# Six even weight places between two attention layers, gelu as one ScalarE instruction, and a norm moved into the stage of w4

## The chip, the core and the metric

The kernel runs on one core of a Trainium2 chip. The core has TensorE (PE: matrix products; its weight loads are shown as PEld), VectorE (DVE), ScalarE (ACT), GpSimd (POOL) and SyncE (SP), and 16 DMA engines that bring data from HBM. All transfers of this kernel are issued on SP's queue, in the order in which the program planned them. The metric is device time in microseconds (us); less is better. The time of a kernel is the median of several runs, and beside it there is one execution that the hardware profiler recorded.

## The reference

A decode step for two sequences (B = 2, one new token each, width D = 576) through two layers. Each layer is an attention over a cache of 16384 keys and values with 32 heads of 128, followed by a block with a small mixing part and an MLP. Both layers use the same weights and the same caches.

```python
def layernorm(x, eps=1e-5): return (x - mean(x)) / sqrt(var(x) + eps)

def A(x):                       # attention, 2 x 32 heads, 16384 keys, Dh = 128
    q = (x @ wq).reshape(B, 1, 32, 128)
    p = softmax(q . k_cache * 128 ** -0.5)
    return (p . v_cache) @ wo   # wq [576, 4096], wo [4096, 576]

def Bmix(x):
    h = gelu(layernorm(x) @ w1)         # w1, w2 [576, 576]
    hs = shifted(h) @ w2                # one token: every shift leaves zeros
    x1 = x + hs
    return x1 + gelu(layernorm(x1) @ w3) @ w4   # w3 [576, 4608], w4 [4608, 576]

x = x + A(layernorm(x));  x = x + Bmix(layernorm(x))    # layer 1
x = x + A(layernorm(x));  x = x + Bmix(layernorm(x))    # layer 2
```

With one token the four shifted groups are all padding, so hs is a product of zeros with w2. The kernel computes it that way, once, and computes h of both layers at the end.

## The kernel before, in words

**Sizes.** There are 64 heads (2 sequences x 32), numbered 0 to 63. The keys of one head are a tile of 4 MB: 128 partitions, in each 128 blocks of 128 bf16 (32 KB). Its values are another such tile. Two layers read 1.09 GB in all. On-chip memory `mem` has six slots of one tile each, numbered 0 to 5.

**One head.** Of its 128 key blocks, half are transposed by TensorE in chunks of 8 blocks (`transposes`, L1225) into one of four PSUM banks `tps`, copied by ScalarE into one of three buffers `kt` (`evacuate`, L1237), and multiplied with q (`scores`, L1251). The other half is multiplied by VectorE with the broadcast q and summed (`dots`, L1271 and L1275). A maximum over partitions follows on GpSimd (L1291), the exponentials on ScalarE (`softmax_exp`, L1300 to L1306), and the products with the values on TensorE (`pv`, L1345). The work of head s is interleaved with the softmax and the value products of head s - 1. Most heads run in a loop.

**Carried heads.** Layer 2 begins with heads 62, 63 and 61. The keys and values of 62 and 63 stay in memory from layer 1 to layer 2, and so does part of head 61. For that the halves of K of heads 62 and 63 that VectorE used are transposed too, sixteen chunks that are written back in place: these are "turned" chunks (`turn`, with TensorE's transposes and, in `settle`, ScalarE's copies). Four of them are turned when head 63 begins, two after the products with w3, and ten behind the chunks named in the table `TURNS`. `park` transposes the first chunks of head 61's keys into the `kt` buffers (`PARKED` = 3), which frees the memory where they lay.

**The stage between the layers.** When attention of layer 1 is done, the products with wo, w3, w4 and (for layer 2) wq follow, each of about 5 MB of weights. Memory is nearly full of carried tiles, so the weights pass through *places*: four of 576 KB in slot 4 (`A[0]` to `A[3]`, where 72 value blocks of head 61 lay) and one, `B`, in slot 1 (where head 61's parked key chunks lay). The planner `Store` keeps transfers in a fixed order; a transfer is issued as soon as its place is free, and none overtakes another. A place is free when TensorE has used the piece in it. wo comes in 8 pieces, w3 in 7 (two of them 1152 KB), w4 in 10, wq in 8 (one of 1024 KB). `rows_projection` (L872) computes the products with wo and w4, `cols_chunk` (L751) and `cols_tail` (L768) those with w3 and wq.

**The dependences.** `layernorm` (L688 to L715) forms sums on VectorE, adds them over partitions with a product with ones (L695), takes a square root on ScalarE (L707) and scales. The first chunks of w3 and wq are multiplied with the raw x, so that they need not wait for the norm, and corrected later (`scaled`). In `z_projection` the norm for w1 (`layernorm("xb", ...)`) stands between the last whole chunks of w3 and its tail. Then z is summed (L906), and `gelu` takes three VectorE operations (L910, L911, L913), a sigmoid on ScalarE (L914) and one more on VectorE (L915). w4 needs its result. After wq, q is written at L814.

**Behind the stage.** `carried` scores heads 62, 63 and 61 from what lies in memory. The 72 value blocks of head 61 are fetched again in four pieces into slot 4, then the keys of head 0 in four quarters into slot 3 (where head 62's keys lay), then tiles of heads 1 and on as slots 5, 0, 2, 1 come free. SP's issues are all at L101.

Of the kernel before, what the change touches and what calls it, by code (L numbers as in the profile page):

```python
# [328 lines left out]
class KB:  # L329
# [42 lines left out]
    def _alloc(self):  # L372
# [23 lines left out]
        self.g_a = self.prod[:, 0:2 * MT * B].bitcast(FP32)  # L396
        self.g_b = self.prod[:, 2 * MT * B:4 * MT * B].bitcast(FP32)
# [14 lines left out]
        w = KT * NL * B  # L412
        hg = self.kt[0][:, :, :].rearrange("p j n -> p (j n)")
        self.hg = [hg[:, 2 * w * i:2 * w * (i + 1)].bitcast(FP32) for i in range(2)]
# [16 lines left out]
    def plan_tile(self, t, u, slot, cuts=()):  # L431

        b, hh = u % self.B, u // self.B
        src = (self.K if t == "k" else self.V)[b, hh].rearrange("(p j) d -> p (j d)", p=128)
        cuts = [0, *cuts, self.NB]
        for a, z in zip(cuts[:-1], cuts[1:]):
            self.plan_piece(t, u, slot, src, a, z - a)

    def plan_piece(self, t, u, slot, src, a, n):
        sem = f"tile{slot}" if n == self.NB else f"piece{slot}_{a}_{n}"  # L440
        self.store.plan((t, u, a, n), sem, slot * self.TILE + 256 * a, 256 * n,
                        [(lambda m: m, src[:, a * 128:(a + n) * 128])])
# [60 lines left out]
    def plan_all(self):  # L503
# [12 lines left out]
        for (t, u), slot in zip(tiles, place):  # L516
# [12 lines left out]
        self.cuts["w4", 0] = [(h + a, h + b, at) for h in (0, MT // 2)  # L529
                              for a, b, at in zip(g[:-1], g[1:], (A[2], A[3], B, A[0], A[1]))]  # L530
        self.plan_rows("wo", 0, self.wo, self.cuts["wo", 0])
        h = MT // 2
        self.plan_cols("w3", 0, self.w3, [(0, 0, h, A[3]), (0, h, MT, B), (1, 0, MT, A[0]), (2, 0, MT, A[2]),
                                          (3, 0, h, B), (3, h, MT, A[0]), (4, 0, MT, A[1])])
        self.plan_groups("w4", 0, self.w4, self.cuts["w4", 0])
        h = H // 2
        self.plan_cols("wq", 1, self.wq, [(0, 0, H, A[2]), (1, 0, h, B), (1, h, H, A[1]), (2, 0, h, A[0]),
                                          (2, h, H, A[2]), (3, 0, h, A[3]), (3, h, H, B), (4, 0, H, A[1])])

        b, hh = third % self.B, third // self.B  # L540
        for i in (0, 2, 3, 1):
            self.plan_piece("v", third, 4, self.V[b, hh].rearrange("(p j) d -> p (j d)", p=128), i * self.GONE // 4,
                            self.GONE // 4)
        tiles = self.tile_order(1)
        place = [(3, 4, 5, 0, 2, 1)[i % 6] for i in range(len(tiles))]
        for i, (t, u) in enumerate(tiles):
            if (t, u) != ("v", third):
                self.plan_tile(t, u, place[i], (quarter, half, half + quarter) if i == 0 else
                               (half,) if i == len(tiles) - 1 else ())
# [134 lines left out]
    def layernorm(self, sk, src, dst, dk, after=None):  # L684
# [9 lines left out]
        tot = self.mps[:, 0:2 * B]  # L694
        self.pe(lambda pe: pe.matmul(tot, lhsT=self.ones_f[:, :],  # L695
                                     rhs=self.stat[:, :, :].rearrange("p a b -> p (a b)"), start=True, stop=True),
                reads=["stat", "ones_f"], writes=["mps"])
        if after:
# [3 lines left out]
                reads=["mps"], writes=["mv"])  # L702
# [37 lines left out]
    def cols_chunk(self, w, l, k, out, pk, n, rhs, rk, cols, first, last=False):  # L740
# [15 lines left out]
        if l == (1 if w == "wq" else 0):  # L756
            self.turn(self.TURNS.get((w, k), 0))

# [35 lines left out]
    def q_projection(self, l):  # L794
# [7 lines left out]
                       after=lambda: self.cols_chunk("wq", l, 0, acc, [ak], n, self.raw[:, 0, 0:w], "raw", cols, True, True))  # L802
# [56 lines left out]
    def rows_projection(self, w, l, rhs, rk):  # L859
# [4 lines left out]
        for i, (a, b, _) in enumerate(cuts):  # L864
# [11 lines left out]
            self.store.release(nm)  # L876
            if l == 0:
                self.turn(self.TURNS.get((w, i), 0))

    def z_projection(self, l):  # L880
# [6 lines left out]
        chunk = lambda k: self.cols_chunk("w3", l, k, acc, [ak], MT, self.raw[:, k, :], "raw", cols, k == 0, k == R - 1)  # L887
# [16 lines left out]
        self.layernorm("xb", self.xb, self.xn2[:, l, :, :], "xn2")  # L904
# [4 lines left out]
    def gelu(self, src, sk, a, ak, b, bk, dst, dk):  # L909
        self.dv(lambda e: e.tensor_tensor(out=a, in0=src, in1=src, op=ALU.mult), reads=[sk], writes=[ak])  # L910
        self.dv(lambda e: e.tensor_scalar(out=a, in0=a, scalar1=GELU_C, scalar2=1.0, op0=ALU.mult, op1=ALU.add),  # L911
                reads=[ak], writes=[ak])
        self.dv(lambda e: e.tensor_tensor(out=b, in0=a, in1=src, op=ALU.mult), reads=[ak, sk], writes=[bk])  # L913
        self.act(lambda e: e.activation(out=a, in_=b, func=ACT.Sigmoid, scale=GELU_S), reads=[bk], writes=[ak])  # L914
        self.dv(lambda e: e.tensor_tensor(out=dst, in0=src, in1=a, op=ALU.mult), reads=[sk, ak], writes=[dk])  # L915

    def gelu_z(self):
        self.gelu(self.z, "prod", self.g_a, "prod", self.g_b, "prod", self.gT, "prod")
# [28 lines left out]
    def attention(self, l):  # L947
# [11 lines left out]
        for s in range(self.CARRY + 1 if l else 0, U):  # L959
# [7 lines left out]
            if still and s == U - 1:  # L967
                self.unturned = [(v, b) for v in o[U - self.CARRY:] for h in range(2)
                                 for b in range(h * self.BP + self.PB, (h + 1) * self.BP, self.CH)]
                self.unsettled = []  # L970
                self.turn(4)
            self.landed(l, "k", u, both=turning)
            after = self.early(l, s - 1)
            for c in range(2 * n):
# [24 lines left out]
                elif s >= 1:  # L999
# [28 lines left out]
        if leave < U:  # L1028
            self.park(o[leave - 1])
# [28 lines left out]
    def turn(self, n, settle=True):  # L1058

        for _ in range(n):  # L1060
            u, b = self.unturned.pop(0)
            self.transposes(0, u, b, 0, self.chunk)
# [10 lines left out]
    def park(self, u):  # L1073

        n = self.PARKED
        self.store.carve(("k", u, 0, self.NB), [self.CH * (i + 1) for i in range(n)] + [self.BP])
        for c in range(n):
            self.transposes(0, u, c * self.CH, c, self.chunk)
            self.store.release(("k", u, c * self.CH, self.CH))
            self.unsettled.append((self.chunk, (None, self.kt[c][:, :, :].rearrange("p j n -> p (j n)"), [("kt", c)])))  # L1080
            self.chunk += 1

    def carried(self, o):
# [13 lines left out]
        def fresh(c):  # L1097
            self.transposes(1, o[2], c * self.CH, c, self.chunk)
            self.evacuate(c, self.chunk, (None, self.kt[c % self.NKT][:, :, :].rearrange("p j n -> p (j n)"),
                                          [("kt", c % self.NKT)]))  # L1100
            self.chunk += 1
# [13 lines left out]
        still(1, 0, 6)  # L1115
        self.softmax_exp(1, 0, o[0])
        dots(1)
        third(3)
        fresh(5)
        still(1, 6, 11)  # L1120
        third(4)
        fresh(6)
        still(1, 11, N)
        self.softmax_max(1, 1, o[1])
# [316 lines left out]
```

## Time and profile before

| quantity | before |
|---|---|
| median of 3 runs | 2559.52 us (2559.41 to 2559.8) |
| the profiled execution: its time / its span | 2557.7 us / 2556.0 us |
| bytes read from HBM | 1092.37 MB, 427 GB/s over the span |
| VectorE / TensorE / ScalarE busy | 74% / 63% / 47% of the span |
| DMA, slices 20 and 21 of 40 (1214 to 1342 us) | 414 and 359 GB/s |

How to read it: the span is cut into 40 equal slices of 64 us; each digit is a busy share in tenths, and GB/s is what the DMA engines moved. A row of a stage gives its start and end, its length, then for each engine its busy time and instructions, TensorE's granted clock, the DMA share and GB/s. In the timeline a row is start, duration, engine, line, operation, out<-in, and in brackets the idle time before it and what ended it. In a view of waits a row is engine, what waited, who ended the wait, total us, times and the longest. The chain of waits is the work that ended last, followed back; its rows are start, duration, what.

### The profile page before, as it was taken

The numbers are of one execution on the slowest core, as the hardware profiler recorded it, in microseconds if no ns is written. First come the engines' busy times: TensorE is split into PE (matmuls) and PEld (weight loads), VectorE is DVE, ScalarE is ACT, GpSimd is POOL, SyncE is SP. The second block draws the span as 40 slices with busy tenths as digits, with TensorE's granted clock in tenths as the row PEclk, the third lists the DMA queues.
The fourth block names the chain that finished last, engine by engine and source line by source line (L and its number), as shares of the span: only waits on it lengthen the run. The fifth ranks groups of instructions, "written<-read, shape, count | busy, mean of one in ns | idle before, by whom it ended". The sixth has DMA issues, their size and how long they took to land.

```text
span 2556.0 us, 74895 instructions
## 1 busy us (share of the span) xinstructions
PE 1616.7 (63%) x34407; PEld 1582.5 (62%) x34407; DVE 1899.1 (74%) x2074; ACT 1200.7 (47%) x1808; POOL 52.5 (2%) x151
## 2 busy tenths in 40 slices
PE   4666666666666666665777666666666666666566
PEld 3666666656656666665667656666665666666566
DVE  5877777777777777777648777777777777777774
ACT  3544444544444454444435544454444445444442
POOL 0000000000000000000000000000000000000000
PEclk8555555555555555555655555555555555555655
DMA  9999999999999999999999999999999999999999
GB/s 410 430 430 433 431 431 432 432 431 431 432 431 432 431 432 433 431 432 432 414 359 427 433 431 431 433 431 432 432 430 434 430 432 433 431 431 432 431 433 388
DMA packets 46496, 1093.19 MB, mean 428 GB/s; under 512 B 5092, under 2 KB 6248, under 8 KB 11624
## 3 DMA queue, kind: packets, MB, share of 16 engines
q1 hardware_dynamic: 46440, 1092.40, 99.9%
q8 instruction: 41, 0.67, 0.1%
q14 instruction: 15, 0.12, 0.0%
HBM read 1092.37 MB, written 0.00 MB: 427 GB/s over the span
## 4 chain that ended last, share of the span: by engine, by line
DMA 66%; DVE 22%; PE 5%; issue 5%; SPq 1%; ACT 1%; DVEq 0%; POOLq 0%
DMA mem<-in_A_k_cache_dram 64%; DVE s_dve L1275 12%; DVE prod L1271 8%; PE tps L1225 2%; PE mps L1345 2%; DMA mem<-in_B_w_dram 2%; SPq L101 1%; PE sps L1251 1%; DMA mem<-in_A_wq_dram 1%; PE sps L1196 1%; ACT mem L1237 0%; DVE diag L1192 0%; DMA mem<-in_A_wo_dram 0%; DVE q_col L1189 0%; DVE l L1323 0%
## 5 line engine op out<-in xcount | busy, mean ns | idle before, releaser
L1237 ACT ACTIVATE kt<-tps 128x1024 bf16<-128x1024 bf16 x992 | 1003.0, 1023 | 878.4 <-PE tps L1225 862.0
L1275 DVE TENSOR_REDUCE s_dve<-prod 128x16 f32<-128x2048 bf16 x504 | 1152.1, 2286 | 17.3
L1225 PE MATMUL tps<-ident,mem 128*128 128x128 bf16 x8192 | 1000.2, 300 | 140.1 <-POOLq L202 134.8
L1271 DVE TENSOR_TENSOR prod<-mem,qb 128x2048 bf16<-128x2048 bf16 x504 | 616.7, 1224 | 533.1 <-POOLq L202 498.1
L1345 PE MATMUL mps<-p,mem 128*128 128x1 bf16 x16384 | 512.1, 165 | 549.6 <-POOLq L202 522.5
L1225 PEld LDWEIGHTS tps<-ident,mem 128*128 128x128 bf16 x8192 | 762.7, 136 | 149.8 <-POOLq L202 144.3
L1345 PEld LDWEIGHTS mps<-p,mem 128*128 128x128 bf16 x16384 | 488.2, 105 | 557.3 <-ACT p L1306 553.7
L1251 PEld LDWEIGHTS sps<-q_col,kt 128*128 128x128 bf16 x7936 | 399.6, 113 | 0.7 <-issue 0.5
L1251 PE MATMUL sps<-q_col,kt 128*128 128x1 bf16 x7936 | 387.8, 170 | 0.6 <-issue 0.4
L1196 PE MATMUL sps<-diag,ones_bf 128*128 128x128 bf16 x127 | 36.5, 288 | 194.1 <-DVE diag L1192 194.1
L1196 PEld LDWEIGHTS sps<-diag,ones_bf 128*128 128x128 bf16 x127 | 13.3, 105 | 204.3 <-DVE diag L1192 204.3
L1300 ACT ACTIVATE mx<-mx 128x1 f32<-128x1 f32 x128 | 26.1, 204 | 233.6 <-POOL mx L1291 233.6
L1199 ACT ACTIVATE qb<-sps 128x128 bf16<-128x128 f32 x127 | 35.2, 277 | 139.2 <-PE sps L1196 139.2
L1291 POOL PARTITION_ALL_REDUCE mx<-mx x128 | 50.1, 392 | 2450.7 <-DVE mx L1289 2321.5
L1237 ACT ACTIVATE mem<-tps 128x1024 bf16<-128x1024 bf16 x32 | 31.3, 1043 | 33.1 <-PE tps L1225 28.0
L1303 ACT ACTIVATE p<-s_dve,mx 128x64 bf16<-128x64 f32 x126 | 43.8, 348 | 4.1
L1306 ACT ACTIVATE p<-sps,mx 128x64 bf16<-128x64 f32 x128 | 37.7, 294 | 0.1
L1286 DVE TENSOR_REDUCE mx<-sps 128x1 f32<-128x64 f32 x128 | 27.6, 216 | 7.5 <-PE sps L1251 7.5
L872 PE MATMUL mps<-prod,mem 128*128 128x2 bf16 x680 | 22.1, 166 | 17.2 <-DMA mem<-in_B_w_dram 7.0
L872 PEld LDWEIGHTS mps<-prod,mem 128*128 128x128 bf16 x680 | 20.2, 104 | 19.5 <-DMA mem<-in_B_w_dram 7.8
L1192 DVE TENSOR_SCALAR diag<-ident,q_f 128x128 bf16<-128x128 bf16 x127 | 31.1, 245 | 0.0
L707 ACT ACTIVATE misc<-misc 128x2 f32<-128x2 f32 x8 | 2.4, 294 | 52.4 <-DVE misc L705 52.4
(122 smaller groups left out, 293.1 us busy)
## 6 DMA issues: line engine op xcount, KB each, us to landing
mem<-in_A_k_cache_dram SPq DMA_DIRECT2D x124, 4096.0 KB, 40.7
mem<-in_A_v_cache_dram SPq DMA_DIRECT2D x123, 4096.0 KB, 49.6
mem<-in_B_w_dram SPq DMA_DIRECT2D x9, 1152.0 KB, 33.4
mem<-in_B_w_dram SPq DMA_DIRECT2D x17, 576.0 KB, 7.3
mem<-in_A_v_cache_dram SPq DMA_DIRECT2D x3, 2048.0 KB, 40.4
mem<-in_A_wq_dram SPq DMA_DIRECT2D x5, 1024.0 KB, 7.0
mem<-in_A_wo_dram SPq DMA_DIRECT2D x8, 576.0 KB, 18.6
mem<-in_A_wq_dram SPq DMA_DIRECT2D x8, 512.0 KB, 6.9
```

The source lines that it names most:

```text
L872: ins = pe.matmul(self.mps[:, t * B:(t + 1) * B], lhsT=buf[:, o:o + 128], rhs=rhs(k), start=(k == 0 and t == 0), stop=(k == last), skip_gr ...
L1196: self.pe(lambda pe: pe.matmul(qps, lhsT=self.ones_bf[:, :], rhs=self.diag[:, :], start=True, stop=True, skip_group_check=True), reads=["o ...
L1199: self.act(lambda e: e.activation(out=self.qb[i][:, :], in_=qps, func=ACT.Copy), reads=[("qps", i)], writes=[("qb", i)], sig=("qb", i))
L1225: ins = pe.transpose(self.tps[t][:, j * 128:(j + 1) * 128], buf[:, j * 128:(j + 1) * 128], self.ident[:, :])
L1237: self.act(lambda e: e.activation(out=out, in_=self.tps[t][:, :], func=ACT.Copy), reads=[("tps", t)], writes=keys, sig=("evac", c, t, k))
L1251: ins = pe.matmul(self.sps[sp][:, c * self.CH + j:c * self.CH + j + 1], lhsT=buf[:, j * 128:(j + 1) * 128], rhs=self.q_col[:, sp:sp + 1], ...
L1271: self.dv(lambda e: e.tensor_tensor(out=prod, in0=buf.rearrange("p (j d) -> p j d", d=128), in1=qbc, op=ALU.mult), reads=[("qb", r)] + key ...
L1275: self.dv(lambda e: e.tensor_reduce(out=sd[:, c0:c0 + DB], in_=prod, axis=AX.X, op=ALU.add), reads=["prod"], writes=[("s_dve", r)], sig=(" ...
L1291: self.pool(lambda e: e.partition_all_reduce(mx[3], mx[2], channels=128, reduce_op=ROP.max), reads=[("mx2", i)], writes=[("mx3", i)])
L1303: self.act(lambda e: e.activation(out=p[:, n:self.NB], in_=self.s_dve[i][:, 0:self.NB - n], func=ACT.Exp, bias=mx[4], scale=self.scale, ac ...
L1306: self.act(lambda e: e.activation(out=p[:, 0:n], in_=self.sps[i][:, 0:n], func=ACT.Exp, bias=mx[4], scale=self.scale, accum_out=self.ls[:, ...
L1345: ins = pe.matmul(self.mps[:, 448:449], lhsT=buf[:, j * 128:(j + 1) * 128], rhs=p[:, col:col + 1], start=b == 0, stop=b == self.NB - 1, sk ...
```

## The change

- The weights get **six places of one size**: four in slot 4 as before and two in slot 1, used in a fixed rotation. Every piece is 576 KB (wq: 512 KB); w3 and wq come in halves of their chunks, so there are 9 pieces of each, and 36 in the stage.
- For the sixth place five chunks of head 61's keys are parked instead of three: three in `kt`, and two, transposed behind the second piece of wo, that stay in two of the four PSUM banks (`full`) until layer 2 copies them out. Other chunks pass over these banks.
- The four turned chunks of the beginning of head 63 move into head 62, ahead of the exponentials of head 61. The table `TURNS` names other chunks. Behind the first wq chunk and the second w3 chunk the copy of the turned chunk is held until the square root of the norm has been issued.
- The **first quarter of head 0's keys** is fetched into slot 1, ahead of the last piece of head 61's values. In `carried` the scores of both carried heads come first, then the rest in another order.
- **gelu is one activation** of ScalarE (tanh approximation), for z and for h.
- The **norm for w1** leaves `z_projection`. It now stands in `rows_projection` behind the third piece of w4 in layer 1 and the second in layer 2, with its sums in bank `sps[0]`.

```diff
-    PARKED = 3
+    PARKED = 5
-    TURNS = {("w3", 0): 1, ("w3", 1): 1, ("w3", 2): 1, ("w3", 3): 1, ("w4", 1): 1, ("w4", 4): 1, ("w4", 7): 1,
-             ("wq", 1): 1, ("wq", 2): 1, ("wq", 3): 1}
+    TURNS = {("w3", 0): 1, ("w3", 1): 1, ("w3", 2): 1, ("w4", 1): 1, ("w4", 3): 1, ("w4", 6): 1, ("w4", 8): 1,
+             ("wq", 0): 1, ("wq", 1): 1, ("wq", 2): 1}
...
-        A, B = [4 * T + P * i for i in range(4)], T
-        assert 256 * self.GONE == 4 * P and 256 * 8 * self.PARKED >= P
-        self.cuts["wo", 0] = [(4 * i, 4 * i + 4, at) for i, at in enumerate((*A, B, *A[:3]))]
+        a, c = [4 * T + P * i for i in range(4)], [T, T + P]
+        assert 256 * self.GONE == 4 * P and 256 * 8 * self.PARKED >= 2 * P and 256 * 8 * self.NKT >= P
+        turn = iter([*a, c[0]] + [a[0], a[1], c[1], a[2], a[3], c[0]] * 6)
+        h = MT // 2
+        self.cuts["wo", 0] = [(i, i + 4, next(turn)) for i in range(0, 32, 4)]
+        halves = lambda n: [(k, m, z, next(turn)) for k in range(self.KT - 1) for m, z in ((0, n), (n, 2 * n))] + \
+                           [(self.KT - 1, 0, 2 * n, next(turn))]
+        w3 = halves(h)
...
+        self.cuts["w4", 0] = [(h * i + p, h * i + q, next(turn)) for i in range(2) for p, q in zip(g[:-1], g[1:])]
...
+        self.plan_cols("wq", 1, self.wq, halves(H // 2))
...
-        for i in (0, 2, 3, 1):
-            self.plan_piece("v", third, 4, self.V[b, hh].rearrange("(p j) d -> p (j d)", p=128), i * self.GONE // 4,
-                            self.GONE // 4)
         tiles = self.tile_order(1)
+        b2, h2 = tiles[0][1] % self.B, tiles[0][1] // self.B
+        for i in (1, 2, 3, None, 0):
+            if i is None:
+                self.plan_piece(*tiles[0], T, self.K[b2, h2].rearrange("(p j) d -> p (j d)", p=128), 0, quarter)
+            else:
+                self.plan_piece("v", third, 4 * T, self.V[b, hh].rearrange("(p j) d -> p (j d)", p=128),
+                                i * self.GONE // 4, self.GONE // 4)
...
         self.layernorm("x", self.x, self.xn, "xn",
-                       after=lambda: self.cols_chunk("wq", l, 0, acc, [ak], n, self.raw[:, 0, 0:w], "raw", cols, True, True))
+                       after=lambda: self.cols_chunk("wq", l, 0, acc, [ak], n, self.raw[:, 0, 0:w], "raw", cols, True, True, True))
+        if l:
+            self.settle()
...
             self.store.release(nm)
+            if (w, i) == ("w4", 2 - l):
+                self.layernorm("xb", self.xb, self.xn2[:, l, :, :], "xn2", bank=0)
             if l == 0:
+                if (w, i) == ("wo", 1):
+                    self.park(self.order(0)[self.U - self.CARRY - 1], self.NKT, self.PARKED)
                 self.turn(self.TURNS.get((w, i), 0))
...
         self.layernorm("x1", self.x1, self.xn, "xn", after=lambda: chunk(1))
+        if l == 0:
+            self.settle()
...
-        self.layernorm("xb", self.xb, self.xn2[:, l, :, :], "xn2")
         self.cols_tail("w3", l, out, [pk], MT, cols)
...
-    def gelu(self, src, sk, a, ak, b, bk, dst, dk):
...
+    def gelu(self, src, sk, dst, dk):
+        self.act(lambda e: e.activation(out=dst, in_=src, func=ACT.Gelu_apprx_tanh), reads=[sk], writes=[dk])
...
+                            if still:
+                                self.unturned = [(v, b) for v in o[U - self.CARRY:] for h in range(2)
+                                                 for b in range(h * self.BP + self.PB, (h + 1) * self.BP, self.CH)]
+                                self.unsettled, self.full = [], ()
+                                self.turn(4)
                             self.softmax_exp(l, s - 1, o[s - 1])
...
+    def park(self, u, a, z):
...
+        for c in range(a, z):
             self.transposes(0, u, c * self.CH, c, self.chunk)
             self.store.release(("k", u, c * self.CH, self.CH))
+            if c < self.NKT:
+                self.unsettled.append((self.chunk, self.chunk_place(c)))
+            else:
+                self.full = (*self.full, self.chunk % self.NT)
             self.chunk += 1
...
+        dots(0)
+        self.softmax_max(1, 0, o[0])
+        still(1, 0, N)
+        self.softmax_exp(1, 0, o[0])
         for c in range(3):
             third(c)
-        dots(0)
-        self.softmax_max(1, 0, o[0])
+        dots(1)
+        self.softmax_max(1, 1, o[1])
         fresh(3)
         fresh(4)
...
```

More of the change, by code (lines that the diff above doesn't have):

```diff
@@ L738, in unscaled, with cols_chunk @@
                 reads=["x", "raw"], writes=["raw"])
-    def cols_chunk(self, w, l, k, out, pk, n, rhs, rk, cols, first, last=False):
+    def cols_chunk(self, w, l, k, out, pk, n, rhs, rk, cols, first, last=False, held=False):
         c = rhs.shape[-1]
@@ L756, in cols_chunk @@
         if l == (1 if w == "wq" else 0):
-            self.turn(self.TURNS.get((w, k), 0))
+            self.turn(self.TURNS.get((w, k), 0), settle=not held)
     def cols_tail(self, w, l, out, pk, n, cols):
@@ L907, in z_projection @@
                 reads=[pk, "prod"], writes=["prod"])
-    def gelu(self, src, sk, a, ak, b, bk, dst, dk):
[L910 to L915, printed above, removed]
+    def gelu(self, src, sk, dst, dk):
+        self.act(lambda e: e.activation(out=dst, in_=src, func=ACT.Gelu_apprx_tanh), reads=[sk], writes=[dk])
     def gelu_z(self):
-        self.gelu(self.z, "prod", self.g_a, "prod", self.g_b, "prod", self.gT, "prod")
+        self.gelu(self.z, "prod", self.gT, "prod")
     def early(self, l, s):
@@ L1061, in turn @@
             u, b = self.unturned.pop(0)
+            while self.chunk % self.NT in self.full:
+                self.chunk += 1
             self.transposes(0, u, b, 0, self.chunk)
```

92 lines of the change are left out of this document (38 added, 54 removed).

## The prediction

> **What bounds the kernel now.** I read the slices of the span first, then the same quantities by stage.
>
> ```profile
> DMA  9999999999999999999999999999999999999999
> GB/s 410 430 430 433 431 431 432 432 431 431 432 431 432 431 432 433 431 432 432 414 359 427 433 431 431 433 431 432 432 430 434 430 432 433 431 431 432 431 433 388
> ```
>
> ```profile
> 1100.00:1200.00 100.00, 62.74 (x1332) 61.54 (x1329) 76.92 (x77) 48.41 (x72) 1.80 (x5) 0.59 1.00 432
> 1200.00:1264.00 64.00, 46.52 (x1015) 44.77 (x1016) 45.80 (x53) 36.44 (x56) 3.48 (x4) 0.61 1.00 425
> 1264.00:1321.00 57.00, 35.53 (x797) 32.36 (x795) 13.43 (x80) 15.32 (x20) 0.00 (x0) 0.50 0.95 347
> 1321.00:1338.00 17.00, 15.31 (x446) 15.15 (x443) 10.99 (x12) 8.63 (x15) 2.50 (x2) 0.50 1.01 405
> 1338.00:1400.00 62.00, 45.12 (x999) 44.28 (x996) 54.65 (x56) 30.37 (x46) 1.05 (x3) 0.56 1.00 429
> ...
> 2520.00:2530.00 10.00, 6.71 (x210) 6.27 (x208) 2.49 (x13) 0.00 (x0) 0.00 (x0) 0.50 1.00 418
> ```
>
> The transfers bound the kernel: in the attention they run at 432 GB/s while the busiest engine (VectorE, third of the pairs) is at 77%. Only time in which they fall below that can be won. The hole is the stage between the layers, 1264 to 1321, where 57.0 us x 347 GB/s = 19.8 MB of weights arrive. The last row is the end of layer 2, where weights stream without waiting for a place: 418 GB/s is what weights can reach. At 418 the stage would take 47.3 us, so 9.7 us are to be won there. Behind it 17.0 x (1 - 405/431) = 1.0 and 62.0 x (1 - 429/431) = 0.3 are missing, 1.3 together.
>
> Why is the rate low? The view of the issuing line in that stage tells how long a transfer takes, the waits of TensorE who it waits for, the chain of waits how the two follow each other:
>
> ```profile
> DMA to landing us min/median/max: 4.8/6.7/7.9
> ```
>
> ```profile
> PE sps L751 <- DMA mem<-in_A_wq_dram: 5.6, 5, 1.7
> PE mps L872 <- DMA mem<-in_A_wo_dram: 3.9, 4, 2.0
> PE mps L872 <- DMA mem<-in_B_w_dram: 3.4, 3, 1.6
> PE mps L695 <- DVE misc L692: 3.0, 3, 1.3
> ...
> PE sps L751 <- DMA mem<-in_B_w_dram: 1.0, 2, 0.6
> ```
>
> ```profile
> 1267.33 6.93 DMA mem<-in_A_wo_dram
> ...
> 1274.31 0.71 PE mps L872 x20
> ...
> 1275.03 6.68 DMA mem<-in_B_w_dram
> ...
> 1281.76 1.34 PE sps L751 x36
> ...
> 1283.12 6.27 DMA mem<-in_B_w_dram
> ...
> 1289.43 0.76 PE sps L751 x18
> 1290.19 0.89 PE tps L1225 x8
> ...
> 1294.54 1.23 PE mps L872 x40
> ...
> 1319.36 0.59 PE sps L751 x16
> ...
> 1321.28 0.23 DVE q_f L814
> ```
>
> TensorE waits for weights (5.6 + 3.9 + 3.4 + 1.0 = 13.9 us), and the weights wait for a place that TensorE frees: issue, about 6.7 us to landing, a short product, the next issue. Five places of 576 KB (0.590 MB) at 347 GB/s turn over once in 5 x 0.590 / 0.347 = 8.5 us: 6.7 under way and 1.8 waiting for or in a product.
>
> **The change part by part.** *The sixth place.* Six places in the same 8.5 us carry 6 x 0.590 / 8.5 = 416 GB/s, about all that weights reach; the stage would be 47.5 us. That is the upper end, since a fuller queue and the pauses of TensorE lengthen the turn. At the longest landing, 7.9, the turn is 9.7 us, 365 GB/s, 54.1 us: the lower end. Between them I followed every piece by hand: it lands 6.7 us after its issue or 1.41 us (0.590/0.418) after the one before, whichever is later; its product takes 0.71 (wo, w4), 0.76 (half of a w3 chunk) or 0.59 us (half of a wq chunk), and each turned chunk 0.89 us of TensorE.
>
> *What pays for the place* is two more parked chunks behind the second piece of wo: 16 transposes, 1.8 us of TensorE, with the third and fourth pieces queued behind them. Two transposes fewer run in layer 2, so the sum over the kernel is nil; in the stage it is +1.8. The two results stay in two of the four PSUM banks, so a turned chunk may wait for the copy of the one before the last (0.93 us, below). Pieces lie between the turns, so I take 0; without that cover it is 10 turns x 0.93 = 9.3 us. TensorE without its waits for weights needs 57.0 - 13.9 + 1.8 = 44.9 us, 2.4 less than the transfers at 418: the transfers stay the bound, narrowly.
>
> *Even halves.* Two pieces of 1152 KB and one of 1024 KB become halves: a place is freed after 0.76 us, not 1.34. There are three more transfers to issue, on a queue that stands waiting for places anyway: 0.
>
> *Gelu on ScalarE and the moved norm.*
>
> ```profile
> 1291.25 0.71 PE L768 MATMUL sps<-xt,mem 128*128 128x4 bf16 x18
> ...
> 1291.82 1.87 PE L1225 MATMUL tps<-ident,mem 128*128 128x128 bf16 x16
> ...
> 1292.33 1.28 ACT L914 ACT_TABLE_LOAD   x1
> ...
> 1292.92 0.23 DVE L906 TENSOR_TENSOR prod<-sps,prod 128x72 f32<-128x72 f32 x1
> ...
> 1293.95 0.26 ACT L914 ACTIVATE prod<-prod 128x72 f32<-128x72 f32 x1 [0.34 <-DVE prod L913]
> ```
>
> From the last product of w3 (1291.96) to the first of w4 (1294.54) pass 2.6 us: the norm for w1 delays L906 to 1292.92, then four short VectorE operations and a sigmoid follow. With the norm gone and one activation (0.26 by the sigmoid's row, at most the 0.93 of a copy of 1024 columns; below zero it can't be, as it stays on this path) z and gelu take 0.3 + 0.3. Late next are the two turned chunks that stand ahead of w4 on TensorE, 1.87 us, so w4 starts about 1.8 behind: 0.8 won. The loads of tables stay as many (gelu's for the sigmoid's) and start as soon as ScalarE is free, as the one here did 1.6 us before its use; uncovered, 1.28. The norm moves behind the third piece of w4: its three sums are long done, its 0.25 us product and its square root lie beside w4's remaining pieces. Uncovered it costs what it cost ahead of L906, 1.0.
>
> *The square root ahead of the copy.*
>
> ```profile
> 1281.75 0.16 DVE L705 TENSOR_TENSOR misc<-misc 128x2 f32<-128x2 f32 x1
> ...
> 1283.99 1.02 ACT L1237 ACTIVATE mem<-tps 128x1024 bf16<-128x1024 bf16 x1 [2.54 <-PE tps L1225]
> 1284.91 0.29 ACT L707 ACTIVATE misc<-misc 128x2 f32<-128x2 f32 x1
> ```
>
> The root's input is there at 1281.91; it starts 3.0 us later, behind a copy. Held back, the copy lets the xn of w3 come 3.0 us sooner; late next is the third chunk's weight. The held copy delays only the next use of its bank.
>
> *The four chunks moved from head 63 to head 62.*
>
> ```profile
> 1233.23 0.20 ACT L1300 ACTIVATE mx<-mx 128x1 f32<-128x1 f32 x1 [3.01 <-POOL mx L1291]
> ...
> 1243.12 11.11 ACT L1237 ACTIVATE mem<-tps 128x1024 bf16<-128x1024 bf16 x12 [0.90 <-PE tps L1225]
> ...
> 1258.55 2.72 PE L1225 MATMUL tps<-ident,mem 128*128 128x128 bf16 x24
> ...
> 1260.13 0.19 ACT L1306 ACTIVATION_READ_ACCUMULATOR p<-sps,mx 128x1 f32 x1
> ...
> 1261.07 1.89 PE L1345 MATMUL mps<-p,mem 128*128 128x1 bf16 x64
> ```
>
> Four of twelve copies (0.93 each, 3.7 us) leave the row at 1243.12 and go where ScalarE waited 3.0 us, so the values of head 61 are read up to 2 us later; the first wo pieces take their place, and these have 20 us to spare. The last value products began 0.8 us after their weights were ready, behind 24 transposes; these now come earlier. So wo starts 0.8 sooner.
>
> *The sum for the stage.* By hand the last product of w3 then ends at 1288.8 (1292.0 before), w4 starts at 1290.6 (1294.5), and q is there at 1315.0 (1321.3): **6.3 us**, between 57.0 - 54.1 = 2.9 and 9.7.
>
> *Behind the stage.*
>
> ```profile
> 1321.77 1.02 PE sps L1251 x32
> ```
>
> ```profile
> 1322.81 12.21 SPq L101 DMA_DIRECT2D mem<-in_A_k_cache_dram  x5
> ...
> 2551.28 1.10 PE L872 MATMUL mps<-prod,mem 128*128 128x2 bf16 x30 [0.82 <-DMA mem<-in_B_w_dram]
> ```
>
> The first row is from the chain, the next two from the timeline. After q, four quarters of a key tile go out at once, but the fifth transfer only at 1335.0, when head 63's keys are read. Now a quarter goes out ahead of q into two weight places, and both carried heads are scored first: 256 products at 1.02 / 32 = 0.03 us each, so the fifth can go out some 8 us after q where it took 13.7. I take the 1.3 us missing there, between 0 and 1.3. One wait is new: the tile for slot 1 waits until that quarter is read, and on the queue the next tiles wait behind it. Two tiles of 4.2 MB (9.7 us each) are then under way; less the 6.7 us to landing, up to 12 us of that wait cost nothing. The last row: the end waits for weights; gelu and norm there win 0 (a load that lost its cover would cost 1.28).
>
> 6.3 + 1.3 = 7.6 us. The profiled execution took 2557.7 us (span 2556.0), 1.8 under the median of 2559.5; 2557.7 - 7.6 = 2550.1 on its scale, **2551.9 us** on the median's.
>
> **The rivals.**
> 1. *Everything hidden.* Weights run at 418 throughout: 9.7 + 1.3 = 11.0, 2548.5 us. For it speaks 416 against 418; against it the pauses at the norms (the waits for L692): a turn of 8.5 us against 6 x 1.41 = 8.46 has no slack to take them up.
> 2. *Places are not what limits, or TensorE becomes the bound.* Then only the start (0.8), gelu (0.8) and the part behind (1.3) count: 2556.6 us. Waiting on PSUM banks comes near it: 44.9 + 9.3 = 54.2 us of stage, 2.8 + 1.3 won, 2555.4. For it speaks TensorE's small margin, against it the 13.9 us for weights.
> 3. *Slower.* More and smaller transfers under way lengthen the landing: at 8.4 us the turn is 10.2 and the rate 347 again; from 9.3 us on it is 319 GB/s, the stage 62 us and, with nothing won elsewhere, the time 2564.5 us and more. For it speaks that 7.9 occurs already, against it that no row shows a landing grow with the number of pieces but by their queueing, and six queued pieces land after 6 x 1.41 = 8.5 us only when they already run at 418 GB/s.
>
> The Trainium skill ("DMA: Bandwidth & Descriptors", section "Anatomy of one DMA", a fit for transfers issued from GpSimd) gives 2.0 us plus bytes / 436 GB/s, so 3.4 us by estimate for 576 KB. By that rule five places would turn over in 5.2 us and outrun the weights already, the sixth would bring nothing, and rival 2 would hold. The trace, whose shortest landing is 4.8, disagrees.
>
> **How the numbers follow.** Forecast 0.60 (2549.5 to 2554), rival 1 0.13, rival 2 0.20, rival 3 0.07. 0.2%, about what a measurement can tell here, is 5.1 us: under 2554.4 is faster, 0.60 + 0.13 = 0.73; rival 2 is the same, 0.20; rival 3 slower, 0.07. The range from 2547.5 to 2557.0 leaves out rival 3 and some of the tails of rivals 1 and 2.
>
> **What would show it.** The slice at 359 GB/s rises above 390; in the stage the rate is near 390 and TensorE's waits for weights fall below 8 us; landings stay near 7. Gelu's gap shrinks to about 1.8 us, filled by transposes; the root follows its input at once. If instead L1225 waits for ScalarE in the stage, it is the banks; if landings exceed 8.4, rival 3; if the rate in the stage stays and TensorE waits on VectorE, rival 2. A new gap at the first tiles of layer 2 would mean that slot 1 is late.

## The result, and the profile after

| | before | changed | difference |
|---|---|---|---|
| median of 6 runs | 2559.5 us (2559.41 to 2561.85) | 2549.9 us (2549.35 to 2551.48) | 9.6 us |
| ratio to the kernel before, 95% interval | | 0.9962 (0.995 to 0.9974) | faster by 0.38% |
| profiled execution: time / span | 2557.7 / 2556.0 us | 2549.84 / 2548.1 us | 7.9 us |

The profiled executions differ by 7.9 us, the medians by 9.6: the recorded execution of the kernel before was 1.8 us below its median, that of the changed kernel lies on its median. What the traces can explain is the 7.9 us.

The slices of the span, after:

```profile
DMA  9999999999999999999999999999999999999999
GB/s 410 428 433 431 432 432 431 433 431 433 430 432 432 432 432 431 433 431 432 419 411 427 432 431 432 432 432 432 432 432 432 432 432 432 432 433 431 433 431 386
```

The slice that stood at 359 GB/s stands at 411; the others differ by at most 5 GB/s. The same quantities by stage, in the same stretches as before (start and end, length, then each engine's busy time, granted clock, DMA share, GB/s):

```profile
1200.00:1264.00 64.00, 47.48 (x1052) 46.08 (x1052) 46.73 (x56) 36.87 (x56) 3.48 (x4) 0.63 1.00 425
1264.00:1321.00 57.00, 40.38 (x946) 37.72 (x942) 17.15 (x81) 18.33 (x23) 1.07 (x1) 0.50 1.02 399
...
1321.00:1338.00 17.00, 11.19 (x328) 10.76 (x329) 9.71 (x10) 6.11 (x11) 1.43 (x2) 0.50 1.03 437
1338.00:1400.00 62.00, 45.59 (x996) 44.59 (x994) 55.38 (x57) 33.63 (x53) 2.42 (x4) 0.61 1.00 428
```

The stage rose from 347 to 399 GB/s: 57.0 us x 52 GB/s = 2.96 MB more by 1321, which at 431 GB/s is 6.9 us. The 17 us behind it rose from 405 to 437: 17.0 x 32 / 431 = 1.3 us. The next stretch is 1 GB/s lower, 0.1 us. 6.9 + 1.3 - 0.1 = 8.1 us, against 7.9 between the spans. The last product with weights of the whole kernel starts at 2543.71 instead of 2551.28, 7.6 us sooner. So all but 0.3 us of the gain lies between 1264 and 1338; the 0.3 arise behind that last product (see the runs on gelu).

Landing times in the stage, and whom TensorE waited for there:

```profile
DMA to landing us min/median/max: 5.3/7.3/11.2
```

```profile
PE mps L874 <- DMA mem<-in_A_wo_dram: 3.6, 4, 1.9
PE mps L695 <- DVE misc L692: 3.0, 3, 1.3
PE mps L874 <- DMA mem<-in_B_w_dram: 2.4, 4, 1.0
...
PE sps L751 <- DMA mem<-in_A_wq_dram: 1.5, 2, 0.9
PE sps L751 <- DMA mem<-in_B_w_dram: 1.0, 2, 0.7
PE sps L768 <- DMA mem<-in_A_wq_dram: 0.9, 1, 0.9
PE sps L768 <- DMA mem<-in_B_w_dram: 0.8, 1, 0.8
```

TensorE still waits 10.2 us for weights (13.9 before). But these are now mostly waits for the transfers' own rate: the DMA engines are covered (share 1.02 instead of 0.95), and the pieces of w3 and w4 land one close behind the other, 1.43 us apart (median; 0.590 MB / 1.43 us = 412 GB/s). The median landing grew from 6.7 to 7.3 us.

The timeline around gelu, and the row of q in the chain of waits, which stood at 1321.28 before:

```profile
1288.61 0.72 PE L768 MATMUL sps<-xt,mem 128*128 128x4 bf16 x18 [0.78 <-DMA mem<-in_B_w_dram]
1289.19 1.87 PE L1241 MATMUL tps<-ident,mem 128*128 128x128 bf16 x16
...
1289.63 0.26 ACT L917 ACTIVATE prod<-prod 128x72 bf16<-128x72 f32 x1 [1.39 <-DVE prod L913]
...
1290.85 1.25 PE L874 MATMUL mps<-prod,mem 128*128 128x2 bf16 x40
```

```profile
1314.12 0.24 DVE q_f L816
```

Gelu took 0.26 us, the sigmoid's time. The two transposes fill the gap ahead of w4, which shrank from 2.6 to 1.5 us (1289.33 to 1290.85).

### The profile page after: what moved, and what is told of

Its sections match the earlier page's. It is cut to its first block, busy times and chain, and to the rows that moved or that the text cites. A ratio compares the mean times of both kernels' runs of the same rounds, so it can differ in the third digit from the quotient of the medians.

```text
span 2548.1 us, 74893 instructions
## 1 busy us (share of the span) xinstructions
PE 1614.7 (63%) x34407; PEld 1580.7 (62%) x34407; DVE 1897.0 (74%) x2062; ACT 1204.2 (47%) x1810; POOL 53.5 (2%) x151
## 4 chain that ended last, share of the span: by engine, by line
DMA 66%; DVE 23%; PE 5%; issue 5%; SPq 1%; ACT 0%; DVEq 0%; POOLq 0%
DMA mem<-in_A_k_cache_dram 63%; DVE s_dve L1291 12%; DVE prod L1287 9%; PE tps L1241 2%; PE mps L1361 2%; DMA mem<-in_B_w_dram 1%; DMA mem<-in_A_wo_dram 1%; PE sps L1267 1%; SPq L101 1%; PE sps L1212 1%; DVE diag L1208 0%; DVE l L1339 0%; DVE q_col L1205 0%; DMA mem<-in_A_wq_dram 0%; DVE mx L1302 0%
## 5 line engine op out<-in xcount | busy, mean ns | idle before, releaser
L1241 PE MATMUL tps<-ident,mem 128*128 128x128 bf16 x8192 | 1000.0, 300 | 141.3 <-POOLq L202 135.2
L1241 PEld LDWEIGHTS tps<-ident,mem 128*128 128x128 bf16 x8192 | 761.3, 136 | 151.1 <-POOLq L202 145.0
```

The costliest lines, as they stand in the source:

```text
L1241: ins = pe.transpose(self.tps[t][:, j * 128:(j + 1) * 128], buf[:, j * 128:(j + 1) * 128], self.ident[:, :])
```

## The experiments

Each run is compared with the kernel before on the same chip. There were three groups on three chips, in which the kernel before had medians of 2559.43, 2560.04 and 2559.65 us. The intervals of the ratios are about 0.0012 to either side, 3 us. So differences of 1 us between these kernels are read from the spans and stages of the profiled executions, and are single readings. Two of the changed kernel gave the same span, 2548.1, but its six executions of the result differ by up to 2.1 us. So a difference of less than 1 us between two spans is not shown to come from the edit, unless rows of the trace say where it arises.

| run | median us | ratio to before (95%) | profiled span us | GB/s 1264-1321 | GB/s 1321-1338 |
|---|---|---|---|---|---|
| before | 2559.5 | 1 | 2556.0 | 347 | 405 |
| changed | 2549.9 | 0.9962 (0.995-0.9974) | 2548.1 | 399 | 437 |
| changed, again | 2550.24 | 0.9965 (0.9952-0.9977) | 2548.1 | 399 | 437 |
| five places | 2554.17 | 0.9977 (0.9967-0.9987) | 2553.0 | 370 | 435 |
| four places | 2560.65 | 1.0003 (0.9993-1.0012) | 2559.1 | 341 | 377 |
| old gelu and norm | 2550.66 | 0.9965 (0.9953-0.9978) | 2548.4 | 400 | 434 |
| before, new gelu and norm | 2559.78 | 1.0 (0.999-1.0009) | 2556.3 | 347 | 409 |
| no early quarter | 2551.62 | 0.9967 (0.9954-0.9979) | 2549.3 | 393 | 436 |
| turned chunks at head 63 | 2550.24 | 0.9965 (0.9951-0.9979) | 2548.0 | 399 | 435 |
| no held copies | 2551.09 | 0.9968 (0.9957-0.9979) | 2548.7 | 397 | 435 |
| second park ahead of wo | 2550.01 | 0.9962 (0.9948-0.9976) | 2547.6 | 401 | 437 |
| before, even halves | 2557.14 | 0.9992 (0.9982-1.0001) | 2555.4 | 368 | 393 |
| changed, old order of scores | 2550.82 | 0.9967 (0.9955-0.9979) | 2549.8 | 401 | 374 |

The theory was: the stage is bound by how often a place turns over, so places set its rate. The rivals: gelu, the norm or the order bring the gain, or the transfers are quick enough for five places.

### Five places, four places

```diff
-        turn = iter([*a, c[0]] + [a[0], a[1], c[1], a[2], a[3], c[0]] * 6)
+        turn = iter([*a, c[0]] * 8)          # five
+        turn = iter([*a] * 9)                # four; head 61's values as 0, 1, 2, the quarter, 3
```

> The changed kernel with one edit: the rotation names five places again (four in slot 4, one in slot 1), all pieces and their order as in the changed kernel, the second place in slot 1 stays empty until the first quarter of head 0's keys. If the number of places times the turn of 8.5 us sets the rate: 5 x 0.590 / 8.5 = 347 GB/s in the stage instead of 399, so 57.0 instead of 49.5 us for its 19.8 MB, less what the smaller pieces save: 5 to 7.5 us slower than the changed kernel, 2555 to 2557.5 us, about 0.9985 of before. If places were not what limits and gelu, norm and order brought the gain: 2550 to 2551 us, 0.9965.

> The changed kernel with four places (those in slot 4), the pieces as they are; head 61's values come back in the order in which these places fall free. If places set the rate: 4 x 0.590 / 8.5 = 278 GB/s, a stage of 71 us, 21 us slower than the changed kernel, 2571 us, 1.0045 of before. If a transfer of 576 KB took the 3.4 us that the fit of the Trainium skill gives (page 'DMA: Bandwidth & Descriptors', section 'Anatomy of one DMA'), four places would turn over in 5.2 us and still carry 454 GB/s: no change, 2550 us.

The stretches of the stage, with five and then four places, and the landing times in it:

```profile
1264.00:1321.00 57.00, 38.80 (x877) 36.00 (x875) 13.51 (x80) 18.50 (x23) 0.00 (x0) 0.50 0.98 370
```

```profile
DMA to landing us min/median/max: 5.2/6.5/8.2
```

```profile
1264.00:1321.00 57.00, 36.09 (x755) 32.68 (x751) 11.90 (x74) 18.29 (x22) 0.00 (x0) 0.50 0.95 341
1321.00:1338.00 17.00, 10.02 (x349) 9.73 (x350) 11.45 (x12) 2.88 (x6) 2.50 (x2) 0.50 0.98 377
```

```profile
DMA to landing us min/median/max: 3.9/5.8/8.2
```

The direction is the theory's: 341, 370, 399 GB/s with four, five, six places, and the spans 2559.1, 2553.0, 2548.1. The rival of the quick transfer, that four places would do as well, is out: four places cost 11.0 us of span. But the size is not the theory's, which had 21 us for four places and 5 to 7.5 for five (4.9 by the spans, 4.3 by the medians). The turn of a place is not a constant 8.5 us. It is 4 x 0.590 / 0.341 = 6.9 us with four, 5 x 0.590 / 0.370 = 8.0 with five, 6 x 0.590 / 0.399 = 8.9 with six. The landing medians carry most of the growth: 5.8, 6.5, 7.3. Part of a landing is waiting behind the other pieces, and that part goes when there are fewer. Each place adds 29 GB/s, not the 69 of a constant turn. These turns count 576 KB for every piece, while the pieces of wq have 512 KB and two of w4 have 288 KB; from one issue into a place to the next into the same place, the traces have medians of 6.5, 7.5 and 8.2 us, which grow in the same way.

The landings show the theory's wait directly. Between two successive weights in the stage, a step of over 2 us occurs seven times with four places, five times with five, and once with six.

### Gelu and the norm, in both directions

```diff
 # changed kernel
-        self.act(lambda e: e.activation(out=dst, in_=src, func=ACT.Gelu_apprx_tanh), reads=[sk], writes=[dk])
+        # four VectorE operations and a sigmoid, as before; layernorm("xb", ...) ahead of cols_tail("w3", ...)
 # kernel before: the reverse
```

> The changed kernel with gelu as before (four VectorE operations and a sigmoid) and the norm for w1 again ahead of the tail of w3, six places as they are. If the places brought the gain: w4 starts 0.8 us later, of which weights hide a part: 0 to 1.5 us slower than the changed kernel, 2550 to 2551.4, 0.9965 of before. If gelu and the norm were needed for it: 4 us slower or more, 2554 us and above.

> The kernel before with only gelu as one activation and the norm for w1 moved into the stage of w4. If places set the rate, w4 starts 0.8 us sooner at most and the kernel gains 0 to 1 us: 2558.5 to 2559.5, 0.9996 to 1.0 of before. If these two edits carry the gain: 4 us or more, 2555.5 and less.

In the changed kernel the old gelu and norm cost 0.3 us of span (0.4 to 0.8 us of median); in the kernel before the new ones win nothing (ratio 1.0). The timeline of the first of these shows why it is so little:

```profile
1288.58 0.75 PE L773 MATMUL sps<-xt,mem 128*128 128x4 bf16 x18 [0.24 <-DMA mem<-in_B_w_dram]
...
1291.49 1.23 PE L879 MATMUL mps<-prod,mem 128*128 128x2 bf16 x40 [0.43 <-DVE prod L926]
```

w4 starts at 1291.49 instead of 1290.85, 0.64 later, and weights that have to come anyway take that up. The 0.3 us of span arise at the very end, at the gelu of h. First the changed kernel, then the one with the old gelu and norm:

```profile
2543.71 1.10 PE L874 MATMUL mps<-prod,mem 128*128 128x2 bf16 x30 [0.68 <-DMA mem<-in_B_w_dram]
...
2547.09 0.22 ACT L917 ACTIVATE h<-h 128x20 f32<-128x20 f32 x1 [6.25 <-DVE h L1409]
```

```profile
2543.69 1.11 PE L879 MATMUL mps<-prod,mem 128*128 128x2 bf16 x30 [0.74 <-DMA mem<-in_B_w_dram]
...
2547.97 0.18 DVE L926 TENSOR_TENSOR h<-h,kt 128x20 f32<-128x20 f32 x1 [0.28 <-ACT kt L925]
```

The last product with weights starts at the same time in both. As one instruction gelu is done at 2547.31, ahead of the end of the span at 2548.1; as five it is done at 2548.15, and the span ends at 2548.4. The gain of the change does not come from these two edits, but for this 0.3 us.

### The early quarter and the order of the scores

```diff
 # no early quarter
-        for i in (1, 2, 3, None, 0):          # None: first quarter of head 0's keys into slot 1
+        for i in (1, 2, 3, 0):
 # old order of scores: the body of carried() from the kernel before
```

> The changed kernel without the early first quarter of head 0's keys: all four quarters go to slot 3 after q, head 61's values come as pieces 1, 2, 3, 0. As I took it, the part behind the stage is worth 1.3 us and the quarter ahead of q is most of it: 0.5 to 1.3 us slower than the changed kernel, 2550.4 to 2551.2. If the order of the scores alone fills that hole: no change. If waiting for slot 1 costs something: faster than the changed kernel.

> The changed kernel with the order of scores, values and dot products at the start of layer 2 as before (head 63 scored in three parts, between other work); the early quarter stays. The fifth transfer behind q then goes out at about 13 us after q instead of 9.5. If two whole tiles under way cover that, as it seems: no change, a span of 2548.1 us. If the order is what fills the hole behind the stage: 1 to 1.5 us slower.

Without the quarter the span is 1.2 us longer, as expected. With the old order it is 1.7 us longer, but that execution lies 0.8 us above the median of its run; by the medians on one chip (2550.82 against 2550.24 us) the old order costs 0.6 us, which is not clear of the scatter. The hole behind the stage is plain all the same. The second fence is the issuing queue with the old order, the third the same row of the changed kernel:

```profile
1321.00:1338.00 17.00, 12.22 (x375) 12.09 (x376) 10.49 (x14) 4.28 (x9) 2.03 (x3) 0.50 0.92 374
```

```profile
1316.86 12.13 SPq L101 DMA_DIRECT2D mem<-in_A_k_cache_dram  x4
```

```profile
1316.61 7.38 SPq L101 DMA_DIRECT2D mem<-in_A_k_cache_dram  x4
```

The fourth transfer of that row, the first whole tile, goes out at the row's end (1329.0, less the 0.3 us of an issue), when head 63's keys are read, and the DMA engines run dry: 374 GB/s. In the changed kernel the row ends at 1324.0, and the tile goes out 5 us sooner.

### Even halves alone

```diff
 # kernel before
-        A, B = [4 * T + P * i for i in range(4)], T
+        a, c = [4 * T + P * i for i in range(4)], [T]
+        turn = iter([*a, c[0]] * 8)
+        # w3 and wq in halves of their chunks, every piece at next(turn); head 61's values as 1, 2, 3, 0
```

> The kernel before with five places of one size and w3 and wq in halves, in rotation; nothing else. The prediction had even halves at 0: then 2559.5 us and 347 GB/s in the stage. The run with five places of the changed kernel (370 GB/s, span 2553.0) leaves 3.0 us of the 7.9 to be explained without the sixth place; if the halves shorten the time that a place is held (1.8 to about 1.5 us), 5 x 0.590 / (6.6 + 1.5) = 364 GB/s and 2 to 3 us faster than before, a span of 2553 to 2554 us.

This run changes the size of the pieces and the rotation of the five places together. In the stage it wins what was expected before it ran; in the stretch behind it loses a little of that again:

```profile
1264.00:1321.00 57.00, 37.71 (x868) 34.26 (x866) 14.44 (x85) 18.20 (x23) 0.00 (x0) 0.50 0.98 368
1321.00:1338.00 17.00, 14.93 (x434) 14.76 (x431) 12.97 (x10) 6.11 (x11) 2.50 (x2) 0.50 1.01 393
```

```profile
DMA to landing us min/median/max: 4.8/6.4/7.7
```

```profile
1320.33 11.81 SPq L101 DMA_DIRECT2D mem<-in_A_k_cache_dram  x5
```

347 to 368 GB/s is 57.0 x 21 / 431 = 2.8 us won by 1321. Five places at 368 GB/s turn over in 8.0 us, of which 6.4 are the landing, so the time in a product and before the next issue fell from 1.8 to 1.6. Behind the stage the rate falls from 405 to 393, since the first whole key tile still waits for head 63's keys, at 1332: 17.0 x 12 / 431 = 0.5 us lost. That leaves 2.3 us, and the medians differ by 2.5 (2557.14 against 2559.65 in the same group). The interval of their ratio reaches just past 1.

The two profiled executions differ by only 0.6. Their issuing queues show where the rest of the lead goes, first of the kernel before, then of this one:

```profile
1346.70 0.33 SPq L101 DMA_DIRECT2D mem<-in_A_k_cache_dram  x1
...
1445.03 0.33 SPq L101 DMA_DIRECT2D mem<-in_A_k_cache_dram  x1
```

```profile
1343.82 0.33 SPq L101 DMA_DIRECT2D mem<-in_A_k_cache_dram  x1
...
1444.63 0.33 SPq L101 DMA_DIRECT2D mem<-in_A_k_cache_dram  x1
```

A lead of 2.9 us at 1344 is 0.4 at 1445, and 0.6 at the end. Yet between the two the DMA engines move the same in both kernels (428 and 429 GB/s from 1344 to 1445), so this loss is not a lower rate: the bytes moved since the start are ahead by 0.9 MB at 1338 and by 1.0 MB at 2500, 2.1 to 2.3 us' worth. What goes is the lead of the last part of each tile. The trace records the landing of a transfer in sixteen parts. In the last whole key tile these parts land 2.35 us sooner on average than in the kernel before, but the last of them only 0.5 us, since they are spread over 5.8 us instead of 3.6, and a tile is used when its last part is there. Why the parts spread differently is open. In the other profiled executions the spread lies between these two. Part of the difference from the medians is the recorded execution of the kernel before, 1.8 us below its median.

The same sum of the two stretches can be made for the other runs. It gives the difference of spans from the kernel before to within 0.6 us for all runs with six places (the changed kernel 8.1 for 7.9, old order 5.9 for 6.2, no quarter 7.3 for 6.7), but 4.2 for 3.0 with five places and -1.9 for -3.1 with four. So with five places or fewer it overstates by 1.2 to 1.7 us, and the spans or medians are to be taken there.

### The smaller parts: turned chunks, held copies, an earlier park

```diff
 # turned chunks at head 63: turn(4) again at the beginning of head 63
 # no held copies
-            self.turn(self.TURNS.get((w, k), 0), settle=not held)
+            self.turn(self.TURNS.get((w, k), 0), settle=True)
 # second park ahead of wo
+            if g == 1 and l == 0:
+                self.park(o[leave - 1], self.NKT, self.PARKED)      # and no park behind the second piece of wo
-        turn = iter([*a, c[0]] + [a[0], a[1], c[1], a[2], a[3], c[0]] * 6)
+        turn = iter([*a, c[0], c[1]] * 7)      # and head 61's values as 0, 1, 2, 3, then the quarter
```

> The changed kernel with the four turned chunks again at the beginning of head 63. As I took it, wo starts 0.8 to 1.0 us later (first product with wo at 1266.0 instead of 1265.0) and the stage ends as much later: 0.8 us slower, 2550.7. If the pieces that wait at the start hide it: no change, 2549.9.

> The changed kernel with the two held copies issued at once, ahead of the square root. As I took it, the xn of w3 comes 3 us later, but its weights are then late as well: 0 to 1 us slower, 2549.9 to 2550.9. If with six places the norm has become the bound: 2 to 3 us slower, 2552 to 2553.

> The changed kernel with the second park between the second and third value product of head 63, ahead of wo, and with the second place in slot 1 taking the sixth piece of wo: it is issued at about 1263.8 instead of 1265.8, while the products with wo start 1.5 us later. In the changed kernel the landings of wo have one gap, 1271.6 to 1274.2, 1.1 us over the usual step. If that gap comes from late issues: 0.7 to 1.1 us faster than the changed kernel, 2549. If it comes from something else or the later start costs as much: 2550 to 2551.

*Turned chunks at head 63:* the first product with wo starts at 1266.47 instead of 1265.04, and the span is the same (2548.0). The pieces that wait at the start hide it, as the other reading in the expectation had it.

*No held copies:* the span is 0.6 us longer. The square root again stands behind a copy, and TensorE waits for the norm:

```profile
1283.44 1.02 ACT L1253 ACTIVATE mem<-tps 128x1024 bf16<-128x1024 bf16 x1 [1.95 <-PE tps L1241]
1284.36 0.29 ACT L707 ACTIVATE misc<-misc 128x2 f32<-128x2 f32 x1
...
1285.29 0.21 PE L725 MATMUL mps<-xn,sel 128*128 128x2 bf16 x2 [1.89 <-DVE xn L715]
```

In the changed kernel L725 runs at 1283.06. Of 2.2 us, 0.6 are left at the end, by one span each.

*Second park ahead of wo:* the issue comes at 1264.24 instead of 1265.76, the products with wo start 2.2 us later (1267.22), and the time is the same (2550.01; span 2547.6). The gap in the landings of wo did not go, it stays at the same time:

```profile
1270.38 0.70 PE L874 MATMUL mps<-prod,mem 128*128 128x2 bf16 x20 [0.70 <-DMA mem<-in_A_wo_dram]
1271.79 0.70 PE L874 MATMUL mps<-prod,mem 128*128 128x2 bf16 x20 [0.72 <-DMA mem<-in_A_wo_dram]
1274.37 0.69 PE L874 MATMUL mps<-prod,mem 128*128 128x2 bf16 x20 [1.88 <-DMA mem<-in_A_wo_dram]
```

The piece behind the gap, the seventh of wo, was issued at 1267.94 here and at 1266.78 in the changed kernel, and landed at 1274.3 and 1274.2. So its time of issue does not set the gap. It is no better version: its ratio is that of the changed kernel.

### The changed kernel again

> The changed kernel as it is, beside the two others on one chip: 2549.9 us, a span of about 2548, 399 GB/s in the stage.

2550.24 us and a span of 2548.1, with the same rates.

## Why the prediction was right

It gave 2551.9 us (2547.5 to 2557.0) and faster with 0.73; the measured median is 2549.9. By its own steps:

- **What bounds: right.** The transfers did, and only where they fell below 432 GB/s. All but 0.3 of the 7.9 us lies in the two stretches that it named.
- **The sum: right on the scale of the profiled executions.** 6.3 in the stage, measured 6.9; 1.3 behind, measured 1.3 less 0.1. It gave 2550.1 us there, and 2549.84 was recorded. The 2 us between prediction and median come from the step that added 1.8 us to go from one execution to the median: the recorded execution of the kernel before was a quick one, that of the changed kernel was not. In part the agreement is luck: gains that the prediction named at single steps (the start of wo, gelu at w4) did not reach the end, and one that it put at 0 (the even halves) was worth up to 2.8 us in the stage.
- **The hand-followed pieces: right to about 1 us.** w3's last product ended at 1289.3 (1288.8 predicted), w4 started at 1290.9 (1290.6), q was there at 1314.1 (1315.0).
- **The turn of 8.5 us as a constant: wrong in form.** It measured 6.9, 8.0 and 8.9 us with four, five and six even places. So the plain ratio (416 GB/s) could not come true; the pieces followed by hand, with 6.7 us to landing or 1.41 us behind the one before, were near, since the measured median is 7.3 and the measured step 1.43.
- **Even halves at 0: wrong.** With five places they raise the stage by 2.8 us' worth of bytes, and the sixth place by 57.0 x 29 / 431 = 3.8 us' worth, by the run with five. The prediction had noted that a place is freed after 0.76 us instead of 1.34, and then priced only the issue of the extra transfers. The 0.76 stands in the pieces that it followed by hand, so its 6.3 us hold both effects; what it did not have is that the halves would gain without the sixth place. What the halves alone are worth at the end lies between 0.6 us (spans) and 2.5 us (medians).
- **Behind the stage: the total right, the parts not.** 1.3 us stood for the quarter and the order together. Taken out one at a time, the quarter costs 1.2 us of span, and the order 1.7 by the spans and 0.6 by the medians. Either way that is more together than the hole that was there before (405 GB/s against 432, 1.1 us); with the old order behind the new stage the hole is larger, 374 GB/s.
- **Gelu and norm: 0.64 us at w4's start for the 0.8, and none of it at the last product.** The cover named (two transposes) is in the timeline. At the end of the kernel, where the prediction had 0, gelu of h as one instruction won 0.3 us of span. In the kernel before, the two edits won nothing. That the loads of tables stay as many was wrong: the traces have 8 before and 10 after, 1.28 us each. One of the new ones stands at 1294.06, ahead of the moved norm's square root; like the norm itself it is covered by the pieces of w4.
- **The start of wo at 0.8: worth 0.** wo started 1.0 us sooner (1265.04 against 1266.07), but its pieces land when they did. The run with turned chunks at head 63 shows that nothing of it reaches the end.
- **The held copies: 0.6 us by one span each**, between the 0 of full cover and the 3.0 of the root's delay.
- **Two PSUM banks kept: right at 0.** No wait of L1241 for ScalarE stands among TensorE's waits in the stage. The slot-1 wait left no hole either: 437 and 428 GB/s behind the stage.
- **Signs foretold:** the slice rose above 390 (411) and the stage's rate is near 390 (399); the waits for weights did not fall below 8 us (10.2). Landings over 8.4 us were to speak for rival 3; single weights took up to 9.0 us, behind others in the queue, and the rate rose all the same.

The Trainium skill's fit for one DMA ("DMA: Bandwidth & Descriptors", section "Anatomy of one DMA") gives 3.4 us for 576 KB by estimate. By that rule four or five places would have been enough. The trace does not agree: four places lost 11.0 us of span against six, with a median landing of 5.8 us. The fit is stated for transfers issued from GpSimd; here they come from SP, several at a time.

## What to carry to other kernels

When weights stream through a few places, ask for three numbers: the bytes of the places, the time to landing, and how long a place is held. But do not take the turn as constant: landing grows with what is queued ahead, so here a place more brought 29 GB/s, under half of what the plain ratio promised. Piece size counts as well as their number, since a place is held for as long as its product runs. And look at what follows a stage that you shorten: with the old order behind the new stage the next big transfer went out 5 us later, and the rate of the 17 us behind the stage fell from 437 to 374 GB/s.

## What the runs showed of the hardware that was not expected

- **Landings of weights keep a step, with one jump.** In the changed kernel and in the run with the earlier park, the sixth and the seventh piece of wo are taken up by TensorE 2.5 to 2.6 us apart, where others are 1.4 apart, each time near 1271.7 to 1274.3. The jump is 1.1 us. In the changed kernel fifteen of the sixteen parts of the seventh piece land at the usual step, by 1273.02, and one lands 1.15 us later. At 1271.11 a packet of 16 KB of the queue for instructions starts, which takes 1.10 us. Twelve of the thirteen profiled executions have such a packet and one late part there (1.2 to 1.6 us late); the one with four places has the packet and the jump, but no single late part. That the packet holds up one of the DMA engines fits this, but is not shown: the traces do not say on which engine a packet ran.
- **Weights stream below the rate of the big tiles.** With the DMA engines covered (share 1.02) the stage stays at 399 GB/s, with key and value tiles 432. The pieces of 576 KB that land 1.43 us apart make 412 GB/s, and the jump above is the only step of over 2 us between weights, so the pauses at the norms leave no gap. A packet of a weight's row (4608 bytes) takes 178 ns in the median, one of 32 KB of a big tile 1215 ns: 25.9 and 27.0 GB/s on an engine, or 414 and 431 on sixteen. That fits the smaller rows as the reason, but no run changed the size of the rows alone.
